# Weight conversion with the exponent shifted earlier and the mask kept in the weight's place, and first products in shared and single banks

## The chip, the cores and the metric

The kernel runs on one core of one Trainium2 chip. The metric is the device time of one execution in microseconds, smaller is better. PE is the matmul engine (TensorE), DVE the vector engine (VectorE), ACT the scalar engine (ScalarE), POOL GpSimd, and SP the engine whose queue issues most of the DMAs.

## What is computed

Two blocks one after the other. The first is a delta-rule attention: for each of 4 batches and 8 heads a 48x48 state is updated over 768 time steps. The second mixes the result with a Fourier transform, normalises it and sends it through two weight matrices.

```python
for t in range(S):                      # q, k, v: (4, 8, 768, 48), beta: (4, 8, 768)
    kt, vt, bt = k_n[:, :, t], v[:, :, t], beta[:, :, t, None]
    y[:, :, t] = einsum('bhd,bhde->bhe', q[:, :, t], state)
    v_old = einsum('bhde,bhd->bhe', state, kt)
    state = state + bt[..., None] * einsum('bhd,bhe->bhde', kt, vt - v_old)
x = y.transpose(0, 2, 1, 3).reshape(4, 768, 384)
u = x + real(fft(fft(x, axis=1), axis=2))
un = (u - mean(u)) / sqrt(var(u) + 1e-6)          # over the last axis
out = u + maximum(un @ w_ch1, 0) @ w_ch2          # w_ch1 384x1536, w_ch2 1536x384
```

The two weight matrices arrive in float64. The kernel turns them into float32 itself, from the two 32-bit words of each number.

## The kernel before

**The attention part** works in chunks of 128 time steps for all 8 heads: `g` counts 24 of them, 6 (`NL`) for each batch `b`. Per chunk it turns the keys and the queries on PE (`turn`, evicted by ACT as KT and QT), makes Gram matrices (evicted by ACT as G and GU) and the masked products of queries and keys (LQ, by DVE, L557), builds the triangular inverse, advances the state (`step`: PE products, with DVE's U, L722, and S, L741, between them) and writes the outputs (x, L764 on ACT and L774 on DVE). The inverses are made for four chunks at a time, a round: `invert16` (L460) is a long chain of small DVE steps that begins with a transpose A (L477) and ends with two transposes (L525, L528). ACT's Z (L610) and MT (L626) read what these write, and PE waits for those.

**The Fourier part** of batch 0 begins with `folds` (L783), eight DVE steps for each of three row pairs (E, O; L797 to L815), then `fourier` (L820): PE products into banks named pf and one, evicted by ACT as F (L859), and for each of six row tiles T a product with dtab, an eviction Q (L875) on ACT, four DVE steps (x, L884 to L887), statistics (bst, mv) and, on POOL, rstd.

**The two weight products** are `mlp` (L902): `normed_of` (un, L913, DVE), `turned` (ptr on PE, unT on ACT), `first_of` (L927: for each of 12 slices fc three matmuls into a bank ph, and an eviction hT with Relu on ACT, L934), and `second_of` (po). Rows go in three groups `g` of 256. PSUM is split into two two-bank buffers "pair", two one-bank buffers "one" and two one-bank buffers "post"; ph, ptr, po and pf use "post", Gram matrices, LQ products and state products use "pair", turns and dtab products use "one". A buffer is handed on when its last reader is done.

**The weights** are converted by `weight` (L224), a generator that runs in 12 pieces for the first matrix and then 12 for the second, each 128x384. For each piece a DMA brings the words into a ring (4 deep for the first, 3 for the second). The steps of a piece i stand in two halves, with a `yield` between them:

- First half: ACT copies the low word as a mantissa part into man (L278); DVE masks the high word into num (L279). ACT then makes, for piece i−1, a power of two from its exponent, with two steps on num (L283, L284).
- Second half: DVE multiplies an earlier piece into its place in the weight (L291; one piece back for the first matrix, two for the second, because the temporaries number two and three), adds the masked part to man (L295), sets the sign (L299), and shifts the exponent out of the high word into num (L301). SP then issues the DMA that refills the ring.

num so holds the mask first and the exponent later.

**The order** is written by hand: all of this is generators that `advance`, `drain`, `convert(n)` (n halves of the weight conversion) and `fill(n)` (n steps of the inversion of round 1, or else of the first eight fold steps) push forward in program order. Inside `manual_schedule` the engines named keep that order. In the stretch that begins with `drain(nq)` (L1307) only PE's order is fixed, and a scheduler places the instructions of ACT and DVE; the weight conversion and the inversion of round 2 are interleaved there. PE, ACT and DVE each take their instructions in order.

The piece of the main program that matters here is: chunks g = 2 to 4 with conversions of the first matrix between the steps (from about 70 us on), the last chunk g = 5 with the folds (to about 113 us), `fourier(0)`, and then a loop over the 12 slices fc of the first group, with one slice, a piece of the Fourier part (after fc 1, 3, 6, 9), a piece of the next chunks' keys and queries, and one piece of conversion (two halves) in each turn (129 to about 167 us):

```python
        for fc in range(KF):
            advance(side)
            if fc in (1, 3, 6, 9):
                advance(f)
            if fc < len(rest):
                advance(rest[fc])
            advance(conv, 2)
```

Then the chunks of batch 1 begin, with the rest of the second matrix's conversion and the inversion of round 2.

Of the kernel before, what the change touches and what calls it, by code (L numbers as in the profile page):

```python
# [10 lines left out]
F32 = mybir.dt.float32  # L11
I32 = mybir.dt.int32
U32 = mybir.dt.uint32
AX = mybir.AxisListType
ALU = mybir.AluOpType
ACT = mybir.ActivationFunctionType
# [48 lines left out]
def kernel(  # L65
# [10 lines left out]
    nc = tc.nc  # L76
# [14 lines left out]
    GT = 2  # L91
# [8 lines left out]
    def ps_pair():  # L100
        return ps.tile([128, 2, 512], F32, tag="pair", bufs=2, name="pair")
# [4 lines left out]
    def ps_post(shape, name):  # L106
        return ps.tile(shape, F32, tag="post", bufs=2, name=name)
# [116 lines left out]
    def weight(last):  # L224

        if moe_w_ch1.dtype == F32:
            if last:
                nc.sync.dma_start(out=w2, in_=moe_w_ch2.rearrange("(c p) m -> p c m", p=128))  # L230
            else:
                nc.sync.dma_start(out=w1, in_=moe_w_ch1.rearrange("(c p) f -> p c f", p=128))
            return
        w1v = moe_w_ch1.bitcast(I32).rearrange("(c p) (f two) -> p c f two", p=128, two=2)
        w2v = moe_w_ch2.bitcast(I32).rearrange("(c p) (m two) -> p c m two", p=128, two=2)
        n = DM
        flat = "p e t m -> p (e t m)"
        if last:
            pieces = [(w2v[:, i:i + 1], w2[:, i:i + 1]) for i in range(KF)]

            E, O3 = spare.pop()
            ring = E.rearrange(flat).bitcast(I32).rearrange("p (i m two) -> p i m two", m=n, two=2)
            tmp = O3.rearrange(flat).rearrange("p (i e m) -> p i e m", e=2, m=n)
            tmp = [tmp[:, i] for i in range(3)]
            deep = 3
        else:
            pieces = [(w1v[:, c:c + 1, i:i + n], w1[:, c:c + 1, i:i + n])
                      for i in range(0, DFF, n) for c in range(KD)]
            ring = wk.tile([128, 4, n, 2], I32, tag="big", bufs=2, name="w64")
            tmp = None  # L250
            deep = 4

        def stage(i):
            if i < len(pieces):
                src = pieces[i][0]
                nc.sync.dma_start(
                    out=ring[:, i % deep].rearrange("p (c f) two -> p c f two",
                                                    c=src.shape[1]), in_=src)

        for i in range(deep):  # L260
            stage(i)
        yield
        if tmp is None:
            tmp = [wk.tile([128, 2, n], F32, tag="M", name="wtmp0"),
                   wk.tile([128, 2, n], F32, tag="unT", bufs=2, name="wtmp1")]

        def of(i):
            t = tmp[i % len(tmp)]
            return ring[:, i % deep, :, 0], ring[:, i % deep, :, 1], t[:, 0], t[:, 1].bitcast(I32)


        lag = len(tmp) - 1
        for i in range(len(pieces) + lag):
            if i < len(pieces):
                lo, hi, man, num = of(i)


                nc.scalar.activation(man, lo.bitcast(U32), ACT.Copy, scale=2.0 ** -52, bias=1.0)  # L278
                nc.vector.tensor_scalar(num, hi, 0xFFFFF, None, op0=ALU.bitwise_and)  # L279
            if 0 < i <= len(pieces):  # L280

                num0 = of(i - 1)[3]
                nc.scalar.activation(num0, num0, ACT.Relu, scale=-1.0, bias=edges[:, 0:1])  # L283
                nc.scalar.activation(num0, num0, ACT.Relu, scale=-2.0 ** 23,  # L284
                                     bias=edges[:, 1:2])
            yield
            if i >= lag:
                _, _, man0, num0 = of(i - lag)
                dst = pieces[i - lag][1]
                c = dst.shape[1]  # L290
                nc.vector.tensor_tensor(dst, man0.rearrange("p (c f) -> p c f", c=c),  # L291
                                        num0.bitcast(F32).rearrange("p (c f) -> p c f", c=c),
                                        op=ALU.mult)
            if i < len(pieces):
                nc.vector.scalar_tensor_tensor(man, num, 2.0 ** -20, man, op0=ALU.mult,  # L295
                                               op1=ALU.add)

                man = man.bitcast(I32)
                nc.vector.scalar_tensor_tensor(man, hi, -2 ** 31, man, op0=ALU.bitwise_and,  # L299
                                               op1=ALU.bitwise_or)  # L300
                nc.vector.tensor_scalar(num, hi, 20, 0x7FF, op0=ALU.logical_shift_right,  # L301
                                        op1=ALU.bitwise_and)
                stage(i + deep)
            yield

# [4 lines left out]
    lo = [slice(64 * e, 64 * e + D) for e in range(2)]  # L310
# [591 lines left out]
    def mlp(b):  # L902

        x, norms = xs.pop(b), normed.pop(b)

        un, hs = {}, {}

        def normed_of(g):

            mv, rstd = norms[g]  # L910
            un[g] = [wk.tile([128, DM], F32, tag="un", bufs=2, name="un") for _ in range(GT)]
            for tt in range(GT):
                nc.vector.tensor_scalar(un[g][tt], x[:, GT * g + tt, :], mv[:, tt, 0:1],  # L913
                                        rstd[:, tt:tt + 1], op0=ALU.subtract, op1=ALU.mult)
            yield

        def turned(g):
            rows = un[g]
            un[g] = wk.tile([128, KD, GT * 128], F32, tag="unT", bufs=2, name="unT")
            for tt in range(GT):  # L920
                pt = ps_post([128, KD, 128], "ptr")
                for dt in range(KD):
                    tr(pt[:, dt, :], rows[tt][:, 128 * dt:128 * dt + 128], dt == 0)
                nc.scalar.activation(un[g][:, :, 128 * tt:128 * tt + 128], pt, ACT.Copy)
            yield

        def first_of(g):  # L927
            hT = hs[g] = wk.tile([128, KF, GT * 128], F32, tag="big", bufs=2, name="hT")
            for fc in range(KF):
                ph = ps_post([128, GT * 128], "ph")  # L930
                for dt in range(KD):
                    mm(ph, w1[:, dt, 128 * fc:128 * fc + 128], un[g][:, dt, :], dt == 0,
                       dt == KD - 1)
                nc.scalar.activation(hT[:, fc, :], ph, ACT.Relu)  # L934
                if b == 0 and g == 0 and fc == 5:
                    drain(normed_of(1))
                yield

        def second_of(g, tt):
            T = GT * g + tt  # L940
            po = ps_post([128, DM], "po")
            for fc in range(KF):
                mm(po, hs[g][:, fc, 128 * tt:128 * tt + 128], w2[:, fc, :], fc == 0,
                   fc == KF - 1)
                if fc % 2 == 1 and fc < KF - 1:
                    yield
            nc.vector.tensor_tensor(x[:, T, :], x[:, T, :], po, op=ALU.add)  # L947
            nc.sync.dma_start(out=out_v[b, T], in_=x[:, T, :])
            yield


        turns = [normed_of(0), turned(0), first_of(0)]
        if b == 0:
            turns += [turned(1), first_of(1), second_of(0, 0), normed_of(2), second_of(0, 1),
                      turned(2), second_of(1, 0), second_of(1, 1), first_of(2)]
        else:
            turns += [normed_of(1), second_of(0, 0), turned(1), second_of(0, 1), first_of(1), normed_of(2),
                      second_of(1, 0), turned(2), second_of(1, 1), first_of(2)]
        for t in turns + [second_of(2, 0), second_of(2, 1)]:
            yield from t  # L960
# [3 lines left out]
    def advance(gen, n=1):  # L964
        for _ in range(n):
            if next(gen, "end") == "end":
                return False
        return True

    def drain(gen):  # L970
        for _ in gen:
            pass
# [121 lines left out]
    with tc.manual_schedule(engines=engines):  # L1094
# [30 lines left out]
        load_q(4)  # L1125
        load_q(5)
        conv = weight(0)
        advance(conv)

# [33 lines left out]
        def fill(n):  # L1163

            while n > 0 and advance(inv1):
                n -= 1
            while n > 0 and advance(fd):
                n -= 1
# [82 lines left out]
        g = NL - 1  # L1251
        c0, c1 = step(g, 0), step(g, 1)
        load_k(g + 2)
        load_v(g + 2)
        advance(c0)
        advance(late)
        advance(c0)
        drain(late)
        drain(keys[0])
        advance(c1)  # L1260
# [11 lines left out]
        f = fourier(0)  # L1272
# [38 lines left out]
    with tc.manual_schedule(engines=engines):  # L1311
        for b in range(1, B):
# [5 lines left out]
            f, then = fourier(b), mlp(b)  # L1318
# [40 lines left out]
```

## Time and profile before

| what | value |
|---|---|
| median of three runs | 753.22 us (750.53, 753.22, 753.52) |
| the profiled execution | 751.29 us |
| its span, first to last instruction | 749.5 us |
| granted TensorE clock, mean over the span | 0.970 |
| PE busy | 691.9 us, 92% of the span |
| PE weight loads busy | 530.3 us, 71% |
| DVE busy | 378.3 us, 50% |
| ACT busy | 263.4 us, 35% |
| POOL busy | 78.7 us, 11% |
| hT, eviction 128x256 (L934) | 144 times, 382 ns each |
| one step of the second matrix's conversion, mean ns, 129 to 175 us | L278 557, L279 355, L283 614, L284 614, L291 547, L295 548, L299 550, L301 353 |
| evictions of 128x512 by ACT (KT, QT), mean ns, 129 to 175 us | 590, 582 |
| weight DMA, 384 KB, from issue to landing, 60 to 200 us | median 3.6 us |

Busy times count how long an engine had an instruction under way. Instructions of one engine overlap a little, so that the next one starts earlier than the duration says: four rows of 0.55 us can start every 0.47 us. In rows of instructions in order of time, a bracket at the end gives how long the engine had stood idle before the row, and what ended the idle time. In the chain of waits, each row is a piece of the chain that ended last: start, length, engine, tile and line.

### The profile page before, as it was taken

The numbers are of one execution on the slowest core, as the hardware profiler recorded it, in microseconds if no ns is written. First come the engines' busy times: TensorE is split into PE (matmuls) and PEld (weight loads), VectorE is DVE, ScalarE is ACT, GpSimd is POOL, SyncE is SP. The second block draws the span as 40 slices with busy tenths as digits, with TensorE's granted clock in tenths as the row PEclk, the third lists the DMA queues.
The fourth block names the chain that finished last, engine by engine and source line by source line (L and its number), as shares of the span: only waits on it lengthen the run. The fifth ranks groups of instructions, "written<-read, shape, count | busy, mean of one in ns | idle before, by whom it ended". The sixth has DMA issues, their size and how long they took to land.

```text
span 749.5 us, 23083 instructions
## 1 busy us (share of the span) xinstructions
PE 691.9 (92%) x10176; PEld 530.3 (71%) x10176; DVE 378.3 (50%) x957; ACT 263.4 (35%) x644; POOL 78.7 (11%) x138
## 2 busy tenths in 40 slices
PE   6877879687999987999999999999999999999998
PEld 4677867566767665878767768877677688777684
DVE  5878778579812797252498229188311241600000
ACT  5545763676514221224312333133223121221120
POOL 8000000100000012021010220030101000200000
PEclk9799899997999998999999999999999999999999
DMA  9842542143123221002322221011210000000000
GB/s 154 219 73 42 123 111 85 23 113 115 35 44 61 56 46 20 12 10 50 56 44 49 41 44 28 1 33 34 44 33 14 12 12 1 22 1 21 11 10 22
DMA packets 108791, 36.10 MB, mean 48 GB/s; under 512 B 101873, under 2 KB 105234, under 8 KB 108690
## 3 DMA queue, kind: packets, MB, share of 16 engines
q1 hardware_dynamic: 106866, 33.86, 20.9%
q8 instruction: 80, 1.31, 0.7%
q0 software_dynamic: 640, 0.43, 0.4%
q10 hardware_dynamic: 1184, 0.33, 0.3%
q14 instruction: 21, 0.17, 0.1%
HBM read 29.88 MB, written 4.72 MB: 46 GB/s over the span
## 4 chain that ended last, share of the span: by engine, by line
PE 77%; DVE 14%; ACT 6%; issue 2%; DMA 0%; SPq 0%; DVEq 0%; ACTq 0%
PE po L110 24%; PE ph L110 23%; PE one L110 15%; PE pair L110 9%; PE one L113 2%; PE unread L1107 2%; DVE M L452 1%; DVE tmp L448 1%; PE ptr L113 1%; ACT wtmp L284 1%; ACT wtmp L283 1%; DVE Z L647 1%; DVE A L407 1%; DVE G L456 1%; PE pf L110 1%
## 5 line engine op out<-in xcount | busy, mean ns | idle before, releaser
L110 PE MATMUL ph<-unT,w 128*128 128x256 f32 x864 | 208.5, 392 | 5.4 <-ACT hT L934 4.7
L110 PE MATMUL po<-w,hT 128*128 128x384 f32 x576 | 206.0, 497 | 0.0
L110 PEld LDWEIGHTS ph<-unT,w 128*128 128x128 f32 x864 | 162.4, 194 | 30.5 <-ACT hT L934 5.6
L110 PEld LDWEIGHTS po<-w,hT 128*128 128x128 f32 x576 | 103.8, 190 | 56.8 <-issue 0.6
L934 ACT ACTIVATE hT<-ph 128x256 f32<-128x256 f32 x144 | 55.0, 382 | 147.7 <-PE ph L110 146.9
L947 DVE TENSOR_TENSOR x<-x,po 128x384 f32<-128x384 f32 x24 | 13.2, 550 | 107.0 <-PE po L110 107.0
L741 DVE TENSOR_TENSOR S<-S,pair 128x192 f32<-128x192 f32 x40 | 14.0, 351 | 72.4 <-PE pair L110 72.4
L884 DVE TENSOR_TENSOR x<-x,one 128x193 f32<-128x193 f32 x24 | 8.5, 355 | 69.3 <-ACT Q L875 69.3
L110 PEld LDWEIGHTS one<-V,MT 64*64 64x64 f32 x768 | 29.6, 139 | 18.8 <-issue 8.6
L110 PE MATMUL one<-V,MT 64*64 64x48 f32 x768 | 34.9, 226 | 2.5 <-issue 1.0
L452 DVE TENSOR_TENSOR M<-M,tmp 128x31 f32<-128x31 f32 (+15 forms) x93 | 35.0, 377 | 3.2
L448 DVE TENSOR_TENSOR tmp<-A,M 128x31 f32<-128x31 f32 (+15 forms) x93 | 33.6, 361 | 2.5
L700 DVE TENSOR_TENSOR V<-V,pair 128x192 f32<-128x192 f32 x33 | 11.6, 351 | 38.3 <-PE pair L110 36.6
L896 POOL TENSOR_SCALAR rstd<-mv 128x1 f32<-128x1 f32 x24 | 6.4, 265 | 227.0 <-DVE mv L892 227.0
L110 PEld LDWEIGHTS one<-dtab,F 97*128 97x128 f32 (+1 forms) x192 | 25.7, 194 | 5.3 <-ACT F L879 0.5
L110 PE MATMUL one<-MT,ND 64*64 64x64 f32 x768 | 28.4, 223 | 1.1 <-ACT MT L649 0.7
L322 ACT ACTIVATE QT<-one 128x512 f32<-128x512 f32 x24 | 14.2, 593 | 38.4 <-PE one L113 38.3
L110 PEld LDWEIGHTS one<-MT,ND 64*64 64x64 f32 x768 | 25.9, 138 | 2.3 <-ACT MT L626 1.1
L568 POOL TENSOR_TENSOR MT<-A,pack 128x512 f32<-128x512 f32 x12 | 12.8, 1066 | 131.7 <-PE one L110 65.8
L110 PEld LDWEIGHTS pair<-U,K 64*64 64x64 f32 x704 | 15.7, 135 | 15.3 <-issue 13.2
L110 PE MATMUL one<-dtab,F 97*128 97x97 f32 (+1 forms) x192 | 26.2, 277 | 0.0
L110 PEld LDWEIGHTS pair<-S,KT 48*64 48x64 f32 x528 | 10.9, 135 | 21.4 <-issue 10.1
(178 smaller groups left out, 1010.2 us busy)
## 6 DMA issues: line engine op xcount, KB each, us to landing
w<-in_moe_w_ch_dram SPq DMA_DIRECT2D x12, 384.0 KB, 5.7
E<-in_moe_w_ch_dram SPq DMA_DIRECT2D x12, 384.0 KB, 3.6
out_dram<-x SPq DMA_DIRECT2D x24, 192.0 KB, 1.9
K<-in_k_dram SPq DMA_DIRECT2D x92, 48.0 KB, 2.3
V<-in_v_dram SPq DMA_DIRECT2D x92, 48.0 KB, 2.2
C<-in_k_dram SPq DMA_DIRECT2D x18, 192.0 KB, 8.9
Q<-in_q_dram SPq DMA_DIRECT2D x18, 192.0 KB, 3.4
w<-in_q_dram SPq DMA_DIRECT2D x6, 192.0 KB, 7.8
```

The lines of the kernel that those rows point to most:

```text
L110: nc.tensor.matmul(o, lhsT=lhsT, rhs=rhs, start=start, stop=stop, skip_group_check=True)
L113: nc.tensor.matmul(o, lhsT=src, rhs=ident[0:src.shape[0], 0:src.shape[0]], is_transpose=True, start=start, stop=True, skip_group_check=True)
L322: nc.scalar.activation(dst.rearrange("p h j t -> p (h j t)"), pt, ACT.Copy)
L448: nc.vector.tensor_tensor(t, A[:, j + 1:W, j:j + 1].broadcast_to([128, n, j + 1]), M[:, j:j + 1, 0:j + 1].broadcast_to([128, n, j + 1]), o ...
L452: nc.vector.tensor_tensor(M[:, j + 1:W, 0:j + 1], M[:, j + 1:W, 0:j + 1], t, op=ALU.add)
L568: nc.gpsimd.tensor_tensor(MT, MTd[:, m8, None, :].broadcast_to([128, 8, 2, W]), m_blk[:, None, :, None].broadcast_to([128, 8, 2, W]), op=A ...
L700: nc.vector.tensor_tensor(R4, R4, pw[:, :, 0:2 * D].rearrange("p a (j e) -> p a j e", e=D), op=ALU.subtract)
L741: nc.vector.tensor_tensor(s1v, s0.rearrange("p h j e -> p h (j e)"), pk, op=ALU.add)
L884: nc.vector.tensor_tensor(near, near, pb[:, 0, 0:MH + 1], op=ALU.add)
L934: nc.scalar.activation(hT[:, fc, :], ph, ACT.Relu)
L947: nc.vector.tensor_tensor(x[:, T, :], x[:, T, :], po, op=ALU.add)
L1107: nc.tensor.matmul(unread[:, 0:DM], lhsT=src[:, 0:128], rhs=src, start=True, stop=True, skip_group_check=True)
```

## The change

It has three parts.

1. In `weight`, the exponent is shifted out of the high word in the first half, together with the mask, half a piece sooner than before. num holds only the exponent; the masked part is written into the piece's own place in the weight matrix (`bits`), from where L295 reads it, and where the product overwrites it later. On ACT the two steps on num stand ahead of the next piece's copy instead of behind it. The product and its operands are written as two-dimensional.
2. In `first_of`, only for the first group of batch 0, the slices fc = 0, 1, 4, 5, 8 and 9 go by twos into the two banks of a "pair" buffer, with one eviction of both by ACT after the second; fc = 2, 3, 6, 7, 10 and 11 go into "post" as before.
3. In the last chunk of batch 0 (g = 5), `fill(2)` stands twice between the steps, so that four more of the first eight fold steps are issued there instead of by the `drain(fd)` that follows.

```diff
@@ weight
         for i in range(len(pieces) + lag):
-            if i < len(pieces):
-                lo, hi, man, num = of(i)
-                nc.scalar.activation(man, lo.bitcast(U32), ACT.Copy, scale=2.0 ** -52, bias=1.0)
-                nc.vector.tensor_scalar(num, hi, 0xFFFFF, None, op0=ALU.bitwise_and)
             if 0 < i <= len(pieces):
                 num0 = of(i - 1)[3]
                 nc.scalar.activation(num0, num0, ACT.Relu, scale=-1.0, bias=edges[:, 0:1])
                 nc.scalar.activation(num0, num0, ACT.Relu, scale=-2.0 ** 23,
                                      bias=edges[:, 1:2])
+            if i < len(pieces):
+                lo, hi, man, num = of(i)
+                bits = pieces[i][1].rearrange("p c f -> p (c f)").bitcast(I32)
+                nc.scalar.activation(man, lo.bitcast(U32), ACT.Copy, scale=2.0 ** -52, bias=1.0)
+                nc.vector.tensor_scalar(num, hi, 20, 0x7FF, op0=ALU.logical_shift_right,
+                                        op1=ALU.bitwise_and)
+                nc.vector.tensor_scalar(bits, hi, 0xFFFFF, None, op0=ALU.bitwise_and)
             yield
             if i >= lag:
                 _, _, man0, num0 = of(i - lag)
...
             if i < len(pieces):
-                nc.vector.scalar_tensor_tensor(man, num, 2.0 ** -20, man, op0=ALU.mult,
+                nc.vector.scalar_tensor_tensor(man, bits, 2.0 ** -20, man, op0=ALU.mult,
                                                op1=ALU.add)
                 man = man.bitcast(I32)
                 nc.vector.scalar_tensor_tensor(man, hi, -2 ** 31, man, op0=ALU.bitwise_and,
                                                op1=ALU.bitwise_or)
-                nc.vector.tensor_scalar(num, hi, 20, 0x7FF, op0=ALU.logical_shift_right,
-                                        op1=ALU.bitwise_and)
                 stage(i + deep)
@@ first_of
             for fc in range(KF):
-                ph = ps_post([128, GT * 128], "ph")
+                wide = b == 0 and g == 0 and fc % 4 < 2
+                if wide and fc % 2 == 0:
+                    both = ps_pair()[:, :, 0:GT * 128]
+                ph = both[:, fc % 2] if wide else ps_post([128, GT * 128], "ph")
                 for dt in range(KD):
                     mm(ph, w1[:, dt, 128 * fc:128 * fc + 128], un[g][:, dt, :], dt == 0,
                        dt == KD - 1)
-                nc.scalar.activation(hT[:, fc, :], ph, ACT.Relu)
+                if not wide:
+                    nc.scalar.activation(hT[:, fc, :], ph, ACT.Relu)
+                elif fc % 2:
+                    nc.scalar.activation(hT[:, fc - 1:fc + 1, :], both, ACT.Relu)
@@ the last chunk of batch 0
         advance(c0)
+        fill(2)
         advance(late)
         advance(c0)
+        fill(2)
         drain(late)
         drain(keys[0])
         advance(c1)
         drain(fd)
```

More of the change, by code (lines that the diff above doesn't have):

```diff
@@ L288, in weight @@
                 _, _, man0, num0 = of(i - lag)
[L289 to L293, printed above, removed]
+                nc.vector.tensor_tensor(pieces[i - lag][1].rearrange("p c f -> p (c f)"), man0,
+                                        num0.bitcast(F32), op=ALU.mult)
             if i < len(pieces):
-                nc.vector.scalar_tensor_tensor(man, num, 2.0 ** -20, man, op0=ALU.mult,
+                nc.vector.scalar_tensor_tensor(man, bits, 2.0 ** -20, man, op0=ALU.mult,
                                                op1=ALU.add)
```

## The prediction

> **What bounds the kernel now.** I read the page first (span and the 40 slices), then the busy time in stretches of 20 us, then the chain of waits, then the engines' instructions in order of time where PE is not full. Columns of the stretches: from:to, length, then busy us (and instructions) of PE, PE's weight loads, DVE, ACT, POOL; then the granted clock, DMA share and GB/s.
>
> ```profile
> span 749.5 us, 23083 instructions
> PE   6877879687999987999999999999999999999998
> ```
>
> ```profile
> 80.00:100.00 20.00, 17.26 (x636) 15.77 (x637) 16.70 (x38) 15.10 (x32) 0.00 (x0) 0.97 0.58 139
> 100.00:120.00 20.00, 14.61 (x373) 13.35 (x369) 16.87 (x40) 8.62 (x21) 0.00 (x0) 1.00 0.30 69
> 140.00:160.00 20.00, 12.66 (x90) 10.21 (x87) 14.67 (x40) 12.90 (x33) 3.32 (x6) 0.91 0.24 54
> 160.00:180.00 20.00, 14.27 (x125) 10.99 (x124) 17.37 (x47) 15.31 (x37) 1.32 (x3) 0.75 0.49 145
> 180.00:200.00 20.00, 20.00 (x215) 15.81 (x215) 18.05 (x59) 10.32 (x25) 0.94 (x1) 1.00 0.23 52
> ```
>
> From 180 us on PE is nearly always busy, so the end comes earlier by what PE gets there earlier. Before that no engine is full: between 140 and 180 us PE works 26.9 of 40 us, DVE 32.0, ACT 28.2. That is a chain of waits, and the chain names it:
>
> ```profile
> 87.11 0.56 DVE w L291
> 87.67 0.48 DVE wtmp L295
> 88.15 0.02 issue
> 88.17 0.56 DVE wtmp L299
> 88.73 0.28 DVE wtmp L301
> 89.01 0.02 issue
> 89.04 0.62 ACT wtmp L283
> 89.66 0.02 issue
> 89.68 0.62 ACT wtmp L284
> 90.31 0.02 issue
> 90.33 0.56 DVE w L291
> ```
>
> One weight piece costs 3.22 us (87.11 to 90.33): four DVE steps, the last of them the exponent's shift (L301), then two ACT steps that need it, then the product that ends the next turn. DVE alone would need 2.1 us a piece (0.56 + 0.48 + 0.56 + 0.28 + 0.27), ACT 1.6 us. The same dance costs PE in the first products of the first group (fc = 0 to 11, one product of 6 rows each):
>
> ```profile
> 144.20 0.63 PE L113 MATMUL one<-pack,C 128*128 128x128 f32 x4 [2.60 <-DVE x L885]
> 149.40 2.93 PE L110 MATMUL ph<-unT,w 128*128 128x256 f32 x6 [3.27 <-ACT hT L934]
> 171.83 0.90 PE L113 MATMUL ptr<-pack,un 128*128 128x128 f32 x3 [4.99 <-ACT hT L934]
> 175.29 5.21 PE L110 MATMUL ph<-unT,w 128*128 128x256 f32 x12
> ```
>
> ```profile
> 147.81 0.61 ACT L283 ACTIVATE wtmp<-wtmp,edges 128x384 int32<-128x384 int32 x1 [4.41 <-DVE wtmp L301]
> ```
>
> PE stands 3.27 us for an eviction hT, which stands behind this L283 on ACT, which stands 4.41 us for a shift that DVE reaches last. After the gaps PE runs at half speed (2.93 us for six rows that take 1.56 elsewhere, 5.21 for twelve that take 2.86).
>
> **What the Trainium skill says.** "TensorE: Matmul & The Clock Gate", Part 1, has ACT and DVE as strict FIFO, and a PE whose clock falls to half after an idle window of about 3.4 us. The trace agrees with both: the hT above waits behind an ACT step it doesn't need, and the slow rows follow gaps of 3.27 and 4.99 us. "PSUM — Partial Sum Buffer", on bank collisions, says that two engines are kept apart on one bank: that is why x (L884), which reads the bank that Q (L875) evicts, starts only after Q (143.08 + 0.32, then 143.44). "ScalarE: Activation LUTs", on what ACT_TABLE_LOAD costs, gives an ACTIVATE with immediates 186 + 0.833·N ns: 613 for 512 columns; the trace has 593 for QT 128x512.
>
> **The change part by part.** I replay the new order of each engine with durations of the trace, in the old times, and say how far each event moves.
>
> 1. *The weight's steps.* Same eight instructions a piece, none added: mask and shift now come together in the first half, the mask into the weight's own place. Each ACT pair needs a shift half a piece old, and stands ahead of the next piece's copy. The copy comes some 1.1 us later, but its user (L295) stands behind a product of 0.5 us that needs the pair, which ends when the copy starts (0.44 effective): nothing. The mask writes a place that nothing reads before the product overwrites it; its write is of the size of the old one (0.35): nothing, bounds 0 to 0.1 us a piece. The refill DMA waits for the sign step (L299) instead of the shift behind it, 0.28 us sooner, in the same place on SP's queue.
>
> 84 to 105 us: relu, relu, copy run 85.38 to 87.0, the product at 86.65 (87.11 before), Z (L647) at 88.15 (88.92), so PE's 89.74 becomes 88.97. One piece later the gain is 1.2 (Z of L610 done 93.6 for 94.8; PE 93.75 for 94.94), at LQ 1.55 (103.0 for 104.57). Then DVE's own order holds: U at −1.3, S at −1.1.
>
> 2. *fill(2) twice at g = 5.* Four fold steps (L805, L808, L810, L813: 0.59 + 0.39 + 0.27 + 0.39 = 1.64 us) go from behind U to before it, into DVE idle of 0.60, 0.69 and 0.57 us. Price: S about 0.3 later than it could be (in the −1.1). Gain: after the last U (106.65 for 107.81) only L815 is left before the second row. Its E (L810) ends 110.6 for 113.33. **Step A: −2.7 us at pf, 113.38.** From there PE is full to 129.3, so it carries.
>
> 3. *First products.* fc 0/1, 4/5, 8/9 go to the pair buffers with one eviction of 128x512 in place of two of 128x256. Price: 0.48 effective (a row of 0.58 to 0.59, next start) against 2 x 0.27: nothing, bounds ±0.1. What moves is who waits. From 129.3, in old times less 2.7:
> - fc 0/1 evicted at 133.35; Q at 133.8; the old copy and waits gone, hT(2) at 137.75 (139.01), hT(3) 141.5 (142.82), Q 141.8 (143.08).
> - x (L885) ends 142.75, C's turn at 142.85 (144.20), fc 5 to 144.75, fc 6 at once, 144.6 (149.40), as its bank was freed at 138.0.
> - hT(4,5) at 144.8, L283 at 146.9, hT(6) 148.45 (153.72), Q 148.75 (153.98); fc 7 147.6, fc 8 149.45, fc 9 151.35; PE waits 0.5 for KT (153.25); fc 10 154.85, fc 11 156.3 (164.08).
> - ACT is now the late one: L284 ends 156.5, hT(8,9) 157.5 to 158.1, Q 158.1 (163.93). QT,KT 158.15.
> - DVE: x 158.4 to 159.5, LQ, bst, the transpose A (1.96) to 162.55, product 162.6 (168.36). **DVE: −5.8 us.**
> - ACT stands for that transpose (nrm), then copy, hT(10) at 163.6; ptr at 163.95 (171.83), ph at 166.0 (175.29). **PE: −9.3 us.** PE's gap before ptr is 4.4 us, so the slow 5.21 stays.
>
> 4. *To the end of round 2's inversion.* In the old run PE's QT,KT at 203.43 waits for S (203.02), which stands on DVE behind the transposes that end at 202.73. DVE is full from 165 on; it has one shift less to do than at the same product before (0.3), and two waits for PE (1.38 and 0.37 us) vanish as PE is ahead. DVE gains 5.8 + 0.3 + 1.7 = 7.8, PE wants 9.3: DVE decides, QT,KT at 195.7. **Step C: −7.7 us instead of −9.3.** Behind it PE and DVE go on as before; the waits for the next inversion (260 to 290 us) start from PE's own grams and shift along.
>
> The sum: 2.7 + 7.7 = 10.4 us. The profiled execution took 751.29 (span 749.5 and 1.8 around it), so 740.9; about 25 hand-overs of 0.02 to 0.04 us that I took at zero add 0.8: **741.7**. The median of the three runs, 753.22, lies 1.9 above the profiled one; the range covers that.
>
> **Rivals.**
> - *A (0.56), the above*: 738 to 744.5.
> - *B (0.26), DVE keeps its waits for Q.* Q keeps its rank on ACT behind evictions and KT; if the four waits of x for Q (2.85, 2.14, 1.55, 1.94) stay, DVE saves between 129 and 165 us only the two for L284 (1.06 + 1.33), and the end moves by 2.7 + 2.4 + 0.3: 745.9. For it: the order of Q among the evictions is unchanged. Against: two of the ACT steps ahead of Q waited 0.77 to 4.41 us for shifts.
> - *C (0.10), no change*: as B, and PE, ahead of DVE, falls to half clock once or twice more; each such start costs 1.4 (2.93 − 1.56) to 2.4 us (5.21 − 2.86): 748.3 to 750.7. For it: the gap of 4.4 us.
> - *D (0.08), slower: the paired eviction holds ACT.* hT(4,5) is one instruction that needs both products; between them stand C's turn and its wait for x on DVE, and ACT, FIFO, has the weight's steps and the next Q behind it: a ring PE, DVE, ACT. Each us held costs one. To end 3.8 slower than before, three such evictions must hold ACT 14.2 us, 4.7 each; at 5.4 each, 757. Against: my replay has 0, 0.5 and 0.
> That the shift is not really earlier is out: in the new order on DVE the shift stands ahead of the product, on ACT the pair ahead of the copy.
>
> **How the numbers follow.** The chances are from how far the replay leaves room: A's steps are all read off, but twelve of them hang on each other. The time is A's. Below 737 would need DVE's bound gone (0.04); the range up to 749 takes in B and half of C: 737 to 749, about 0.8. A measurement of this kernel tells no change from change at about 0.5% (3.8 us). A, B and a little of C are faster by more: 0.83; within: 0.09; slower: 0.08.
>
> **What would show it.** Right: no ACT L283-like step waits over 1 us for a shift between 84 and 165 us; pf's second row starts near 110.7; fc 6 follows fc 5 at once; the largest PE gap is before ptr, behind nrm and the transpose A; QT,KT near 193 in the new times waits for S on DVE. Wrong: hT from a pair late on ACT with PE idle behind it (D); x still standing 2 us for Q each time (B); QT,KT waiting with PE at half clock (C). The forecast falls if DVE's transposes at the end of round 2 come less than 6 us sooner.

## The result

The changed kernel took 742.86 us (median of 4 runs, 741.86 to 743.66) where the kernel before took 752.14 beside it (4 runs, 750.53 to 753.52): ratio 0.988, 95% interval 0.985 to 0.990, so faster by 1.0 to 1.5%. The profiled execution took 743.66 us, with a span of 741.9.

The page of the changed kernel, its span and PE's row of the 40 slices:

```profile
span 741.9 us, 23087 instructions
PE   6878789969999978999999999999999999999998
```

The eighth to tenth slice, 130 to 186 us, read 9, 6, 9; before they read 6, 8, 7. One of the two holes is left. The same five stretches of 20 us, columns as in the prediction:

```profile
80.00:100.00 20.00, 16.69 (x633) 15.26 (x627) 17.71 (x42) 15.04 (x31) 0.00 (x0) 1.00 0.54 134
100.00:120.00 20.00, 16.74 (x455) 15.28 (x449) 17.88 (x43) 8.98 (x22) 0.00 (x0) 1.00 0.37 86
140.00:160.00 20.00, 17.55 (x196) 14.40 (x191) 17.35 (x48) 17.41 (x42) 3.32 (x6) 1.00 0.43 104
160.00:180.00 20.00, 14.80 (x124) 11.26 (x122) 17.97 (x52) 15.03 (x36) 1.32 (x3) 0.74 0.41 120
180.00:200.00 20.00, 19.08 (x248) 14.53 (x249) 17.76 (x49) 8.59 (x20) 0.85 (x1) 1.00 0.17 33
```

Between 140 and 160 us PE now works 17.55 us instead of 12.66, DVE 17.35 instead of 14.67, ACT 17.41 instead of 12.90: most of the time in which each waited for the next has been filled. Between 160 and 180 PE is where it was (14.80 for 14.27, clock 0.74 for 0.75), while DVE is busy for 17.97 of the 20 us. PE in order of time (start, length, work, idle time before it and what ended it), first two rows of the kernel before, then the changed kernel:

```profile
129.32 1.56 PE L110 MATMUL ph<-unT,w 128*128 128x256 f32 x6 [0.58 <-ACT unT L924]
...
203.43 0.69 PE L110 MATMUL pair<-QT,KT 48*64 48x64 f32 x32
```

```profile
143.98 1.46 PE L110 MATMUL pair<-unT,w 128*128 128x256 f32 x6
145.27 1.46 PE L110 MATMUL ph<-unT,w 128*128 128x256 f32 x6
...
164.22 0.90 PE L113 MATMUL ptr<-pack,un 128*128 128x128 f32 x3 [4.11 <-ACT hT L936]
...
167.56 5.12 PE L110 MATMUL ph<-unT,w 128*128 128x256 f32 x12
...
197.08 0.69 PE L110 MATMUL pair<-QT,KT 48*64 48x64 f32 x32 [0.67 <-DVE S L739]
```

fc 6 follows fc 5 at once (145.27, before 149.40 behind 3.27 us of idle time), ptr comes at 164.22 (before 171.83), and the product QT,KT behind the inversion at 197.08 (before 203.43), where it waits for DVE. The gap of 4.11 us and the slow rows of 5.12 us behind it are left. In the kernel before, the chain of waits from ptr to QT,KT ran over PE, whose slow rows stand near its head (issue is time in which the profile shows no wait):

```profile
175.36 5.14 PE ph L110 x12
...
202.55 0.84 PE pair L110 x48
203.39 0.04 issue
203.43 0.69 PE pair L110 x32
```

In the changed kernel it ends on DVE; the chain of waits of the changed kernel reads:

```profile
192.90 2.12 DVE G L523
195.02 1.49 DVE A L526
196.50 0.16 issue
196.66 0.37 DVE S L739
197.08 0.69 PE pair L110 x32
```

Yet the start went the other way: fc 0 begins at 129.75 us (before 129.32). So this execution gained nothing up to fc 0, 6.8 us from there to QT,KT, and 1.3 us after it. It had started late: its first conversion step on DVE, ahead of which the change does nothing, came 2.9 us later (74.44, before 71.51). The experiments separate these.

### The profile page after: what moved, and what is told of

It is laid out like the page before. It is cut to its first block, busy times and chain, and to the rows that moved or that the text cites. A ratio compares the mean times of both kernels' runs of the same rounds, so it can differ in the third digit from the quotient of the medians.

```text
span 741.9 us, 23087 instructions
## 1 busy us (share of the span) xinstructions
PE 689.6 (93%) x10176; PEld 529.3 (71%) x10176; DVE 377.1 (51%) x957; ACT 262.5 (35%) x641; POOL 79.1 (11%) x138
## 4 chain that ended last, share of the span: by engine, by line
PE 75%; DVE 15%; ACT 6%; issue 2%; DMA 1%; DVEq 0%; ACTq 0%
PE po L110 24%; PE ph L110 21%; PE one L110 15%; PE pair L110 9%; PE one L113 2%; DVE M L450 1%; DVE tmp L446 1%; PE ptr L113 1%; PE unread L1111 1%; DVE tmp L517 1%; DVE M L520 1%; DMA C<-in_k_dram 1%; DVE Z L645 1%; DVE S L739 1%; DVE w L292 1%
## 5 line engine op out<-in xcount | busy, mean ns | idle before, releaser
L110 PE MATMUL ph<-unT,w 128*128 128x256 f32 x828 | 197.2, 390 | 0.0
L110 PEld LDWEIGHTS ph<-unT,w 128*128 128x128 f32 x828 | 155.1, 193 | 23.2
L936 ACT ACTIVATE hT<-ph 128x256 f32<-128x256 f32 x138 | 52.8, 383 | 144.2 <-PE ph L110 143.3
L951 DVE TENSOR_TENSOR x<-x,po 128x384 f32<-128x384 f32 x24 | 13.2, 551 | 107.0 <-PE po L110 107.0
L110 PEld LDWEIGHTS one<-V,MT 64*64 64x64 f32 x768 | 31.1, 143 | 20.0 <-issue 7.7
L110 PE MATMUL one<-V,MT 64*64 64x48 f32 x768 | 36.4, 230 | 4.2 <-DVE V L698 2.6
L110 PEld LDWEIGHTS pair<-U,K 64*64 64x64 f32 x704 | 15.5, 134 | 15.5 <-issue 13.2
```

Of the source, the lines that this page charges most:

```text
L110: nc.tensor.matmul(o, lhsT=lhsT, rhs=rhs, start=start, stop=stop, skip_group_check=True)
```

## The experiments

The first row of fc 0 and QT,KT behind the inversion are the same two PE instructions in every kernel. They cut each profiled execution into three stages. The times of the runs are medians; the ratios are to the kernel before, run beside each. The sixth column adds up the waits that DVE's rows show between fc 0 and the S that QT,KT needs (those under 0.15 us are not listed). The recorded expectations call the fill part 2 and the pairs part 3, as the prediction does.

| kernel | median us | ratio, 95% interval | fc 0 at | fc 0 to QT,KT | waits of DVE in it | from there to the end |
|---|---|---|---|---|---|---|
| before | 752.14 | 1 | 129.32 | 74.11 | 13.2 | 546.1 |
| changed | 742.86 | 0.988, 0.985 to 0.990 | 129.75 | 67.33 | 7.3 | 544.8 |
| changed, again | 743.83 | 0.989, 0.986 to 0.993 | 128.59 | 66.58 | 6.5 | 544.8 |
| part 1 alone | 745.94 | 0.992, 0.990 to 0.995 | 131.41 | 65.89 | 5.8 | 545.0 |
| pairs alone | 751.72 | 0.999, 0.997 to 1.001 | 129.03 | 74.15 | 13.3 | 546.0 |
| fill alone | 749.95 | 0.996, 0.994 to 0.998 | 130.60 | 73.19 | 12.5 | 545.2 |
| changed without pairs | 745.56 | 0.990, 0.986 to 0.993 | 131.84 | 66.87 | 6.7 | 545.1 |
| changed without fill | 746.29 | 0.992, 0.989 to 0.995 | 130.05 | 65.93 | 5.9 | 543.1 |
| shift early, old ACT order | 748.40 | 0.992, 0.990 to 0.994 | 133.82 | 68.01 | 7.4 | 546.1 |
| new ACT order, late shift | 757.74 | 1.006, 1.003 to 1.009 | 134.07 | 78.57 | 16.6 | 545.8 |
| changed, norms on POOL | 743.96 | 0.989, 0.985 to 0.993 | 131.54 | 66.30 | 6.1 | 545.1 |
| changed, sign step twice | 751.43 | 0.997, 0.995 to 1.000 | 132.36 | 72.14 | 8.2 | 545.9 |
| changed, fc 10/11 paired | 744.17 | 0.990, 0.987 to 0.993 | 130.12 | 66.86 | 6.4 | 545.6 |
| the same, norms on POOL | 745.06 | 0.992, 0.988 to 0.995 | 132.02 | 66.20 | 5.7 | 545.0 |

The last column lies within 1.3 us in all executions but one, and no edit reaches there. The fourth column spreads over 5.5 us, and over 3.8 between kernels that are the same up to there. The middle stage is the one that can be read from a single profile, to about 1.5 us: the changed kernel's two executions are 0.75 us apart, and the one without fill, whose code behind fc 0 is the same, is 1.4 from the first.

What is left of the middle stage without DVE's waits is 60.0 to 61.0 us in all kernels but two: 62.0 with the new ACT order and the late shift, 64.0 with the sign step twice, which has 3.8 us of work more. So this stage is as long as DVE's work and DVE's waits in it, and of the 6.8 and 7.5 us that the changed kernel gained there 5.8 and 6.6 are waits of DVE that are gone. In the kernel before 2.1 us of DVE's waits were for PE, behind ptr; in the changed kernel none is.

### Part 1 alone

The `weight` part of the diff on the kernel before, nothing else.

> Part 1 alone (shift half a piece sooner, mask in the weight's place, the pair of relus ahead of the next copy; single evictions and the old fill). My theory: it carries nearly all of step B and C; only fill's 1.5 us of step A is missing, and fc 6 follows fc 5 without a gap even with a single eviction of hT(4), since the relus ahead of it no longer wait for a shift. From 752.1: minus about 8, 744 to 746. Rival 1 (the pairs carry the gap before fc 6): the 3.3 us gap stays, 748 to 750. Rival 2 (the parts only work together): 750 or more.

Measured: 745.94 us, stage 65.89. PE in order of time:

```profile
145.41 2.76 PE L110 MATMUL ph<-unT,w 128*128 128x256 f32 x12
...
155.31 2.74 PE L110 MATMUL ph<-unT,w 128*128 128x256 f32 x6 [1.71 <-ACT hT L932]
...
166.08 0.55 PE L113 MATMUL ptr<-pack,un 128*128 128x128 f32 x3 [1.60 <-ACT hT L932]
```

fc 5 and fc 6 are one run of twelve rows at 145.41, with single evictions. The gap before fc 6 needs no other bank to go: the eviction had stood on ACT behind two relus (L283, L284) that waited for a shift. Without pairs fc 9 waits 1.71 us for an eviction, and PE then arrives later at ptr, where it has less to wait (1.60 instead of 4.11). Rivals 1 and 2 fall.

### The pairs alone

```diff
+                wide = b == 0 and g == 0 and fc % 4 < 2
+                if wide and fc % 2 == 0:
+                    both = ps_pair()[:, :, 0:GT * 128]
+                ph = both[:, fc % 2] if wide else ps_post([128, GT * 128], "ph")
...
+                if not wide:
+                    nc.scalar.activation(hT[:, fc, :], ph, ACT.Relu)
+                elif fc % 2:
+                    nc.scalar.activation(hT[:, fc - 1:fc + 1, :], both, ACT.Relu)
```

> Part 3 alone (paired evictions for fc 0/1, 4/5, 8/9; old weight steps, old fill). My theory: PE's gap before fc 6 goes, but ACT still stands about 4 us for the late shift with Q behind it, so DVE's x and the transposition come when they did: 752, between -1 and +0.5. Rival 1: a third of step B comes from the pairs, 748 to 750. Rival 2: the paired eviction holds ACT, 753 to 757.

Measured: 751.72 us, stage 74.15 against 74.11. ACT's wait and PE, in order of time:

```profile
147.74 0.61 ACT L283 ACTIVATE wtmp<-wtmp,edges 128x384 int32<-128x384 int32 x1 [4.41 <-DVE wtmp L301]
```

```profile
146.43 2.61 PE L110 MATMUL ph<-unT,w 128*128 128x256 f32 x6
...
203.18 0.69 PE L110 MATMUL pair<-QT,KT 48*64 48x64 f32 x32
```

With the pair's banks PE does fc 6 at 146.43, 3 us sooner, and nobody gains by it: ACT still waits 4.41 us for the same shift, to the hundredth, with Q behind it, and DVE waits 13.3 us in the stage, as before. An idle gap that was filled on PE moved the end by nothing, because the waits of ACT and DVE for each other set it. Neither rival's range holds 751.72.

### The fill alone

```diff
         advance(c0)
+        fill(2)
         advance(late)
         advance(c0)
+        fill(2)
         drain(late)
```

> Part 2 alone (two fills of two fold steps ahead of the last U). My theory: the four fold steps of 1.64 us fit into DVE's idle time before U, and the first product of the fold's result comes 1.3 to 1.6 us sooner: 750.5 to 751. Rival: the waits for the next convert piece fill the room and the steps push it back: 752 or a little more.

Measured: 749.95 us; the interval is 0.2 to 0.6% faster. The expected 1.5 us lies in it, and so do 4. Its 22 runs spread from 746.9 to 755.1 us, with a mean granted clock of 0.975 to 0.979 in the eight below 748 and 0.957 to 0.968 in the seven above 752.8: the spread goes with the clock that PE was granted.

### The changed kernel without pairs, and without fill

> The changed kernel without its pairs (parts 1 and 2). My theory: the pairs are worth 0 to 1 us, as hT(10) and the transposition of the next inversion decide the gap before ptr and DVE's order decides the end: 742.5 to 744. Rival: without pairs fc 6 or fc 9 waits for single evictions and passes its wait on to Q and x: 746 to 748.

> The changed kernel without its two fills (parts 1 and 3). My theory: only the fold's four steps come back behind the last U, 1.5 us: 744.5 to 745.5 on the scale of 753 for the kernel before, PE standing about 2 us for E ahead of the first products as before, stage from fc 0 to QT,KT 66.5 to 67.4. Rival (the fill is worth twice that, as the run with the fill alone has it in its median): 746 to 747.

Without pairs: ratio 0.990, as the changed kernel, stage 66.87 between its two; the median of six runs, 745.56, lies above what was expected, and runs of 741.6 and 742.0 are among them. No gain or loss from the pairs shows. Without fill: 746.29, 2.5 to 3.4 us above the changed kernel's two medians and in the rival's range, though the intervals of the ratios overlap, with E late again ahead of the first products (PE waits 1.30 us; 0.42 in the changed kernel, 2.03 before). Its stage, 65.93, is below the changed kernel's 67.33: in this execution the twelve rows behind ptr took 3.72 us instead of 5.12, and DVE waited 0.58 us for the copy instead of 2.0 (more on that wait below). The fill ends before fc 0, and the changed kernel's second execution lies between the two (4.36 us), so I put this down to chance and not to the fill.

### The two halves of part 1

The early shift with the copy still ahead of the relus (with the two-dimensional product, which takes 0.55 us as before), and the relus ahead of the copy with the shift still late:

```diff
                 nc.scalar.activation(man, lo.bitcast(U32), ACT.Copy, scale=2.0 ** -52, bias=1.0)
-                nc.vector.tensor_scalar(num, hi, 0xFFFFF, None, op0=ALU.bitwise_and)
+                nc.vector.tensor_scalar(num, hi, 20, 0x7FF, op0=ALU.logical_shift_right,
+                                        op1=ALU.bitwise_and)
+                nc.vector.tensor_scalar(bits, hi, 0xFFFFF, None, op0=ALU.bitwise_and)
             if 0 < i <= len(pieces):
...
-                nc.vector.scalar_tensor_tensor(man, num, 2.0 ** -20, man, op0=ALU.mult,
+                nc.vector.scalar_tensor_tensor(man, bits, 2.0 ** -20, man, op0=ALU.mult,
...
-                nc.vector.tensor_scalar(num, hi, 20, 0x7FF, op0=ALU.logical_shift_right,
-                                        op1=ALU.bitwise_and)
```

```diff
-            if i < len(pieces):
-                lo, hi, man, num = of(i)
-                nc.scalar.activation(man, lo.bitcast(U32), ACT.Copy, scale=2.0 ** -52, bias=1.0)
-                nc.vector.tensor_scalar(num, hi, 0xFFFFF, None, op0=ALU.bitwise_and)
             if 0 < i <= len(pieces):
...
+            if i < len(pieces):
+                lo, hi, man, num = of(i)
+                nc.scalar.activation(man, lo.bitcast(U32), ACT.Copy, scale=2.0 ** -52, bias=1.0)
+                nc.vector.tensor_scalar(num, hi, 0xFFFFF, None, op0=ALU.bitwise_and)
             yield
```

> Half of part 1 on the kernel before: the shift comes with the mask in the first half and the mask goes to the weight's place, but ACT keeps the copy ahead of the two relus. My theory: the place of the shift is what gains; the copy's 0.44 us ahead of the relus costs a little where ACT is late: 745 to 748, the stage from the first row of fc 0 to QT,KT behind the inversion 66 to 68 us (before: 74.1). Rival: the gain needs the relus ahead of the copy: 750 to 753, stage above 72.

> The other half of part 1 on the kernel before: on ACT the two relus stand ahead of the next piece's copy, DVE's order and the shift's place are the old ones. My theory: the relus still wait for the late shift, so nothing moves: 752 to 754, stage 74 to 75. Rival (ACT's order is what gains): 745 to 749, stage below 71.

The early shift alone: stage 68.01, six of the eight us that part 1 gains there; 748.4 us is 0.4 above what was expected. The new order alone was expected to do nothing and costs 4.4 us (757.74 beside 753.35), 0.3 to 0.9% slower, the stage 4.5 longer. That expectation was wrong, and its rival too. DVE and ACT of that kernel, with their waits:

```profile
165.01 0.56 DVE L295 SCALAR_TENSOR_TENSOR O<-O 128x384 f32<-128x384 int32 x1 [1.03 <-ACT O L284]
...
168.20 0.56 DVE L295 SCALAR_TENSOR_TENSOR O<-O 128x384 f32<-128x384 int32 x1 [1.03 <-ACT O L284]
```

```profile
166.47 0.61 ACT L277 ACTIVATE O<-O,edges 128x384 int32<-128x384 int32 x1 [0.74 <-DVE O L301]
```

L284 is the copy here. ACT waits 0.74 us for the late shift (L301), does two relus, then the copy, and only then can DVE add (L295): 1.03 us in each of these two pieces. In the old order the copy was done while the relus waited. DVE waits 3.4 us longer than before in all: 2.1 for the copy, 1.6 for relus ahead of products, 0.9 for Q and 0.9 for a DMA, less the 2.1 for PE, which went. With the late shift, then, the new order costs 4.4 us. With the early one it seems to gain: the stage goes from 68.01 to 65.89, with 1.6 us less of waits of DVE, half of them for Q and half for PE. That is one execution of each; between the early shift alone and all of part 1 the ratios, both 0.992, show no difference.

### Does DVE decide the end of the inversion?

First by adding work to it:

```diff
+                if last and i >= 4:
+                    nc.vector.scalar_tensor_tensor(man, hi, -2 ** 31, man, op0=ALU.bitwise_and,
+                                                   op1=ALU.bitwise_or)
```

> The changed kernel with the sign step (L299, 0.47 us from one start to the next) done twice for the last eight pieces of the second weight, which lie on DVE between the inversion's start and its end: 3.8 us of work more that changes no value. My theory (DVE decides the end of round 2's inversion, with PE 0.7 us behind): the transpositions and QT,KT come 3.3 to 4 us later, stage 70 to 71 for 66.6 to 67.3, time 746.5 to 748. Rival (PE's chain decides, DVE has room): stage below 68.5, time below 745.

Measured: stage 72.14, 4.8 to 5.6 us longer for 3.8 us of work, 751.43 us. PE in order of time:

```profile
181.98 0.68 PE L110 MATMUL pair<-S,KT 48*64 48x48 f32 x16 [3.37 <-DVE S L740]
182.59 5.49 PE L110 MATMUL ph<-unT,w 128*128 128x256 f32 x12
...
204.50 0.69 PE L110 MATMUL pair<-QT,KT 48*64 48x64 f32 x32 [0.30 <-DVE S L742]
```

All of the added work arrives: without DVE's waits the stage is 3.9 us longer. The rest, 1 to 1.8 us, is waiting, 8.2 us for 7.3 and 6.5: among it 0.70 us for a weight DMA, and 0.77 for PE, which had been left waiting 3.37 us for S and did the next twelve rows in 5.49 us (2.86 at full clock). The rival (DVE has room) falls. The expectation was too low all the same: the time is 7.6 to 8.6 us above the changed kernel's, more than the stage explains, and where the rest arises stays open. Then by taking work away:

```diff
-                nc.vector.tensor_scalar(un[g][tt], x[:, GT * g + tt, :], mv[:, tt, 0:1],
-                                        rstd[:, tt:tt + 1], op0=ALU.subtract, op1=ALU.mult)
+                eng = nc.gpsimd if b == 0 and g > 1 else nc.vector
+                eng.tensor_scalar(un[g][tt], x[:, GT * g + tt, :], mv[:, tt, 0:1],
+                                  rstd[:, tt:tt + 1], op0=ALU.subtract, op1=ALU.mult)
```

> The changed kernel with the two norms un of the third group (0.47 + 0.98 us on DVE at 186.6 us) on POOL. My theory (DVE decides the end of round 2's inversion): the transpositions and QT,KT come 1.1 to 1.5 us sooner, stage 66.0 for 67.3, time 1 to 1.5 below the changed kernel. Rival 1 (PE decides): QT,KT stays, stage 67.3. Rival 2: DVE is held while POOL works on the same memory, stage 67.3 or more, and DVE's steps beside POOL's are longer.

> The changed kernel again, beside the others on one chip: 742 to 744, stage 67.3 within 0.5, with the start up to the first weight piece as far from that of the kernel before in either direction as two executions of one kernel are.

Stage 66.30, only 0.3 below the second execution of the changed kernel, which itself lies 0.75 from the first where 0.5 was expected. POOL and DVE:

```profile
166.63 4.96 POOL L912 TENSOR_SCALAR un<-x,mv,rstd 128x384 f32<-128x384 f32 x2 [0.53 <-PE ptr L113]
```

```profile
168.64 0.65 DVE L288 TENSOR_SCALAR w<-E 128x384 int32<-128x384 int32 x1
...
170.14 0.51 DVE L487 TENSOR_TENSOR bn<-bn,A 128x32 f32<-128x32 f32 x1
...
188.72 0.80 DVE L520 TENSOR_TENSOR M<-M,tmp 128x128 f32<-128x128 f32 x1
```

Beside POOL's 4.96 us the mask takes 0.65 us (0.35 in the changed kernel), bn 0.51 (0.21), a sign step 0.68 (0.49): 0.8 us comes back. And one DVE step beside POOL's V (L629) is longer in each of three kernels: tmp (L519) 0.92 for 0.29 us in the kernel before, one un 0.98 for 0.47 in the changed kernel (187.21 us), M (L520) 0.80 for 0.29 here. So the norms took less from DVE than the 1.4 us expected, and without its waits the stage is 60.2 us, no shorter than the changed kernel's 60.0 and 60.1. Rival 2 had the mechanism right, though not its stage (67.3 or more). The Trainium skill, "GPSIMD Engine Reference", section 1, has the engine's SBUF interfaces shared with VectorE, in contention with DVE steps of two SBUF inputs among others. The trace agrees in part: M and bn are such steps, but so are the product (0.54 us at 169.21) and the add (0.54 at 169.68), which took no longer beside POOL.

### fc 10 and 11 in a pair too

```diff
-                wide = b == 0 and g == 0 and fc % 4 < 2
+                wide = b == 0 and g == 0 and (fc % 4 < 2 or fc > 9)
```

> The changed kernel with fc 10 and 11 in a pair buffer too, so that ptr no longer waits for hT(10) behind the transposition A on ACT. My theory: the gap of 4.1 us before ptr shrinks below 2.5, the twelve rows behind it take 2.9 us in place of 5.1, the copy (L285) no longer stands behind an eviction that waits for slow rows, DVE's wait of 0.5 to 1.5 us for it goes: stage 65.5 to 66.3, time 0.5 to 1.5 below the changed kernel. Rival 1: the pair buffer is late for fc 10 and PE loses there what it gains: stage 66.6 to 67.5. Rival 2: the paired eviction holds the next ones on ACT: above 67.5.

> As the run with fc 10 and 11 paired, and the norms un of the third group on POOL: takes 1.4 us from DVE while PE is no longer late. My theory: the two gains add, stage 64.3 to 65.2, time 1.5 to 2.8 below the changed kernel (741 to 742 on the scale of 753 for the kernel before). Rival: another wait takes their place (PE or ACT), stage 66 or more.

Measured: stages 66.86 and 66.20, both in the range of a rival (rival 1 for the first), times as the changed kernel's within their intervals. PE of the first:

```profile
158.94 4.54 PE L110 MATMUL pair<-unT,w 128*128 128x256 f32 x12 [2.42 <-ACT hT L938]
...
164.53 0.82 PE L113 MATMUL ptr<-pack,un 128*128 128x128 f32 x6
...
175.94 0.45 PE L110 MATMUL pair<-S,KT 48*64 48x48 f32 x16 [3.29 <-DVE S L737]
```

The gap before ptr is gone, as intended, and the rows behind it are fast (2.86). But the pair buffer is late (2.42 us, and a half-clock start), ptr comes at about the same time, and 11 us later PE waits 3.29 us for DVE. As far as these two runs show, PE's gap had been slack. No version here beats the changed kernel.

## Why the prediction was right, step by step

741.7 us was forecast; the profiled execution took 743.66, and the two medians, 742.86 and 743.83, lie 1.2 and 2.1 above the forecast.

- **Step A, −2.7 us at pf.** In the first execution it came: counted from the first conversion step, pf's second row came 2.74 us sooner (39.13 us after it, before 41.87). The kernel before and then the changed kernel, DVE and PE of each:

```profile
71.51 0.36 DVE L279 TENSOR_SCALAR wtmp<-w 128x384 int32<-128x384 int32 x1
...
113.38 0.57 PE L110 MATMUL pf<-evt,E 128*97 128x193 f32 x2 [2.03 <-DVE E L810]
```

```profile
74.44 0.36 DVE L286 TENSOR_SCALAR wtmp<-w 128x384 int32<-128x384 int32 x1
...
113.57 0.57 PE L110 MATMUL pf<-evt,E 128*97 128x193 f32 x2 [0.42 <-DVE E L808]
```

  It was not sure to arrive. The second execution gained 0.77 us over the same way, and four other kernels with the same code up to there from 0.14 us gained to 1.95 lost. In these five executions PE stopped for 2.1 to 2.3 us for reasons that the profile doesn't show (see the last section), in the first and before for 0.5, and in some of them rows at pf ran slow. These stops I didn't have at all. The whole time went down by 8.1 to 9.3 us by the two ratios and the middle stage by 6.8 to 7.5, which leaves 0.6 to 2.5 for A and for what came behind QT,KT. Of A's parts the fill looks larger than my 1.5 (2.9 us by its ratio, 1.3 to 4.5) and part 1 smaller than the rest (5.7 us by its ratio in all, less than its stage gained); that stays open.
- **Step B, DVE −5.8 us.** Counted from fc 0, the product behind the transposition A came 6.0 us sooner (33.03 us after fc 0, before 39.04). Of x's four waits for Q two went (3.07, 1.95, none, 0.29 for 2.85, 2.14, 1.55, 1.94): rival B, which kept all four, falls.
- **Step B, PE −9.3 us.** ptr by itself was right (8.0 us sooner against fc 0 where 7.9 was replayed), but ph came only 8.2 sooner: I let 2.05 us pass from ptr to ph; it is 3.34, and 3.46 before.
- **"Nothing" for the copy behind the relus** is the term that failed. I looked at the product that hides it in the hand-ordered stretch. Behind fc 11 the scheduler orders ACT, and this is what the changed kernel has there, ACT and then DVE:

```profile
172.71 0.39 ACT L936 ACTIVATE hT<-ph 128x256 f32<-128x256 f32 x1 [1.80 <-PE ph L110]
172.99 0.61 ACT L277 ACTIVATE O<-O,edges 128x384 int32<-128x384 int32 x1
173.50 0.55 ACT L285 ACTIVATE O<-E 128x384 f32<-128x384 uint32 x1
```

```profile
168.10 0.56 DVE L295 SCALAR_TENSOR_TENSOR O<-w,O 128x384 f32<-128x384 int32 x1 [0.58 <-ACT O L285]
...
174.08 0.56 DVE L295 SCALAR_TENSOR_TENSOR O<-w,O 128x384 f32<-128x384 int32 x1 [1.45 <-ACT O L285]
```

  The eviction waits for one of the slow rows behind the gap before ptr, a relu and the copy stand behind it, DVE's add behind the copy: 2.0 us of new waits, 1.05 in the second execution (0.59 and 0.46), none in part 1 alone and with fc 10 and 11 paired, where the rows behind ptr were fast. Without them the stage would be 65.3 and 65.5 us, 8.6 to 8.8 below the 74.11 before: more than the 7.7 of step C, so this miss and a gain that I had too small partly cancelled.
- **Step C, −7.7 us, because DVE decides.** DVE does decide (QT,KT waits 0.67 us for S; added work arrives in full), but counted from fc 0 it gained 6.8 and 7.5 us. The two waits for PE that I let vanish did; the copy's waits took most of what this gave. PE stood ready 0.7 us early at QT,KT, not 1.6. One reading was wrong: in the kernel before QT,KT did not wait for S, which had itself waited 0.30 us for PE (203.02 us); PE decided the end of the stage there, as the chain shows, and DVE does only since the change.
- **The pairs.** Priced at nothing, and no gain or loss from them shows. But the prediction leant on them for the gap before fc 6 ("as its bank was freed"), and that gap goes without them. Rival D, in which they hold ACT, falls with the pairs alone (751.72 us).
- **The signs that I named.** fc 6 followed fc 5 at once, the largest gap of PE was the one before ptr, and QT,KT waited for S on DVE. But L277, the relu that was L283, still waits 1.71 us for a shift in both executions (147.78 and 146.60 us), where I allowed 1; pf's second row came at 113.57 and 112.41 instead of 110.7, and QT,KT at 197.08 and 195.17 instead of 193. The transposes at the end of round 2, whose coming less than 6 us sooner was to end the forecast, came 5.9 us sooner in the first execution and 7.8 in the second (the last one begins at 194.90 and 193.00, before 200.79): by this sign the first execution, which had started late, just misses. Counted from fc 0 it is 6.3 and 7.1 us.

So A was the right case: part 1 carries the middle stage, the fill probably one to four us before it, the pairs nothing. How close 741.7 came is luck in part. By QT,KT the two executions were 6.4 and 8.3 us ahead of the kernel before, where 10.4 was forecast less the hand-overs; another 1.3 came behind it, where I forecast nothing and no edit reaches.

## What to carry to other kernels

A gap on an engine names who is waiting, not who is late: before giving it another bank, follow the thing it waits for along its own in-order queue to the instruction there that stands for someone else. When a step is reordered on one engine because its input comes sooner, the two edits have to be judged together: here the new order without the early input made the kernel slower. And a term priced at nothing because something hides it must be looked at again wherever another order (here a scheduler's) holds.

## What was not expected of the hardware

**PE stops within a row, often at the same instruction.** In the fill-alone kernel, PE's lines with idle time that nothing explains, and the counts between them:

```profile
93.67 0.45 PE L110 MATMUL one<-MT,ND 64*64 64x64 f32 x9 [1.53 <-issue]
...
102.03 0.25 PE L110 MATMUL pair<-U,K 64*64 64x48 f32 x1 [1.45 <-issue]
111.50 0.77 PE L110 MATMUL pair<-U,LQ 64*64 64x48 f32 x18 [1.01 <-issue]
```

```profile
93.60:102.00 8.40, 6.26 (x255) 5.84 (x254) 5.44 (x12) 5.23 (x12) 0.00 (x0) 1.00 0.54 133
102.00:111.45 9.45, 5.68 (x255) 4.92 (x256) 8.35 (x21) 6.03 (x15) 0.00 (x0) 1.00 0.43 89
```

From stop to stop lie 255 matmuls and 254 to 256 weight loads, some 510 instructions. Most other profiles stop at one or both of the first two places, for 0.2 to 1.5 us; between 80 and 130 us they add up to 0.5 us in the kernel before and in one execution of the changed kernel, 2.2 in its other one, and 4.0 here. The Trainium skill, "Runtime: NRT & Kernel Launch", on instruction fetch mechanics, says that instructions are fetched in blocks of 256, at a cost that is mostly hidden. Two such blocks fit the distance; if that is what PE waits for, the cost isn't hidden here. That fetching is the cause was not tried.

**A gap's length alone doesn't decide the clock.** Behind 2.60 us of idle time the kernel before ran fc 5 at full speed (1.46 us), behind 1.71 part 1 alone ran fc 9 at half (2.74 us), behind 1.60 its ptr rows were fast again (0.55). The Trainium skill, "TensorE: Matmul & The Clock Gate", Part 1, has an idle window of about 3.4 us; in these traces that is no safe distance, and the 3.27 us that the prediction took as agreeing with it already lay below.
